# A fused decay attention and squared-ReLU MLP: lower halves kept in the next pair's place, row sums and the split of v moved

## The chip, the cores and the metric

The kernel runs on one core of a Trainium2 chip. The metric is device time in microseconds (us). Engines are named as in the profile: PE (TensorE matmul), PEld (its weight loads), DVE (VectorE), ACT (ScalarE), POOL (GpSimd) and SP (SyncE, which here only issues DMAs).

## The reference

Inputs are q, k, v of shape (8 batches, 8 heads, 576 positions, 64) and a forget factor f per position. Per head:

```
scores = q @ k.T / sqrt(D)
cum    = cumsum(log(clip(f, 1e-4, 1)))
scores = where(causal, -1e9, scores + cum[:, None] - cum[None, :])
attn   = softmax(scores)
out    = attn @ v
```

The heads' outputs side by side are x, 4608 tokens by 512, and the result is `relu(x @ w_in)**2 @ w_out` with 2048 hidden columns. All of it is float32.

## The kernel before, in words

**Two streams on one PE.** Attention is walked head by head (64 heads), each head in six units (`UNITS`, keys x queries): u0 is keys 0-127 with queries 256-575, u1 to u3 are the key tiles from 256, 384 and 512, u4 is keys 128-255 with queries 128-575, u5 is keys 0-127 with queries 0-255. One unit is one slot of the main loop (line 762), so a head has six slots. A slot traces `score` of its unit (matmuls into PSUM, exp on ACT, the triangle cut out by POOL's affine select), then `av_part` of the unit two slots earlier (LAG), then what `finish` and the table of events hold for it, and fills up with half steps of the MLP. Two heads make a pair, whose outputs fill the 128 partitions of one place of an `xt` tile; four pairs make a batch.

**The MLP** works on chunks of 256 tokens. One step is a hidden tile of 128: its first half, `mlp1`, is 12 matmuls of 256 columns, then on ACT a ReLU and two squares (`r`, `g`, `gh`), then on DVE the low part `gl`; its second half, `mlp2`, is six matmuls of 512 columns for the step before. `fill` (line 682) traces half steps at the middle and at the end of each slot, so many that their count keeps to a straight line. From `ready[b]`, the slot in which batch b's last pair is finished plus two, it goes from one batch's chunks to the next in 48 slots. Six of the seven lines (two chunks per batch) have 64 half steps for 48 slots: 4/3 per slot, so in three slots four of the six half slots hold a half step and two hold none. One batch has three chunks and two half steps in every slot. The last three chunks follow after the attention.

**From head 14 on** (`NWHOLE`) a probability tile is split into a high and a low part: `ph` (a cast on ACT, line 414), `pl` (a subtraction on DVE, 415). `sum_p` adds the tile to a running total on DVE (428), and after u4 and u5 `columns` reduces the total to row sums (434). The total is also the tile into which u0's and u5's exp writes. v is split likewise by `split_v`: a cast on DVE (321), then a subtraction on POOL (322).

**Row maxima.** Before a head's scores its row maxima are needed, six matmul and DVE pieces (`max_unit`, lines 336 and 342) traced in the head before, at the slots 2.5, 3, 3.5, 4, 4.5 and 5 (`MAXIMA`). A tile of 128 maxima goes by a 512-byte DMA on SP (line 347, `rk<-tcol`) into row 66 of the operand `r2` of the score matmul (line 381). The first score of a head, u0, reads the maxima of queries 256 to 575: the first three of the five DMAs. On the same SP stands `load` (line 250): the next head's q and k, 288 KB, into the only `qkraw` tile, which waits for POOL's last reading of it (line 314).

**Accumulators.** For a split head the output of ph times (v high, v low) has 128 rows, 64 high and 64 low. `av_part` copies the upper 64 rows into `xt` (line 502) and the lower 64 into `xl` (line 504), which is a single buffer named `den`. The accumulator itself is one PSUM bank, so the matmuls of the next part of a head (line 464) wait for both copies.

**Finishing a pair** (`finish`, at the slots of `DIVIDE` after the pair's last): the sums of both heads are stored to DRAM (454) and loaded back in another layout (526, part 0); part 1 adds `xl` to the pair's `xt` place (535), reduces and inverts the sums (537, 540) and stores them (542); part 2 loads them spread over the partitions into the tile `den` (549); part 3 multiplies (551, POOL). The `den` of part 2 and the `xl` of the pairs share the one buffer, and the next pair's first copy into `xl` comes two slots after part 3.

PE, ACT, DVE and POOL run in the order of tracing. SP's order is chosen by the Tile scheduler. A head starts at its u0 score; in what follows an even head opens a pair and an odd head closes it.

Of the kernel before, what the change touches and what calls it, by code (L numbers as in the profile page):

```python
# [9 lines left out]
F32 = mybir.dt.float32  # L10
# [26 lines left out]
def decay_attention_relu2_kernel(  # L37
# [277 lines left out]

    def split_v(h):
        if NWHOLE <= h < NH:
            st = state[h]
            vr = st["vr"][:, :, :D]
            v = st["vhl"] = vhls[h % 2]  # L320
            nc.vector.tensor_copy(out=v[:, :, :D], in_=vr)
            nc.gpsimd.tensor_tensor(
                out=v[:, :, D:], in0=vr, in1=v[:, :, :D].bitcast(F32), op=ALU.subtract,
            )

# [81 lines left out]
    def split_p(h, u):  # L407
        st = state[h]
        j, q0, q1 = UNITS[u]
        n = q1 - q0  # L410
        p = st["p"][u]
        ph = wk.tile([P, 448], F32R, name="ph", bufs=3)
        pl = wk.tile([P, 448], F32R, name="pl", bufs=3)
        nc.scalar.copy(out=ph[:, :n], in_=p[:, :n])  # L414
        nc.vector.tensor_tensor(  # L415
            out=pl[:, :n], in0=p[:, :n], in1=ph[:, :n].bitcast(F32), op=ALU.subtract,
        )
        st["p"][u] = ph, pl
        sum_p(h, u, p)

    def sum_p(h, u, p):

        st = state[h]
        _, q0, q1 = UNITS[u]
        total = totals[0]

        def add(p, q0, q1):
            nc.vector.tensor_tensor(  # L428
                out=total[:, q0:q1], in0=total[:, q0:q1], in1=p, op=ALU.add,
            )  # L430

        def columns(o, q0, q1):
            n = (q1 - q0) // 32
            nc.vector.tensor_reduce(
                out=st["sums"][:, o:o + n], in_=total[:, q0:q1].rearrange("p (i c) -> p c i", c=n),
                axis=mybir.AxisListType.X, op=ALU.add, apply_transpose=True,
            )

        if 0 < u < NU - 1:
            add(p[:, max(QA - q0, 0):q1 - q0], max(q0, QA), q1)  # L440
            if q0 < QA:
                st["rest"] = p[:, :QA - q0], q0, QA
        if u == NU - 2:
            st["sums"] = wk.tile([P, NC], F32, name="sums")
            columns(0, QA, S)
        if u == NU - 1:
            add(*st.pop("rest"))
            columns(NH1, 0, QA)

# [16 lines left out]
    def av_part(h, u, low):  # L466
# [21 lines left out]
        if last:  # L488
            n = QA if low else S - QA
            if not low:  # L490
                if h % H == 0:
                    xts[h // H] = wk.tile([P, NCC, S], F32, name=f"xt{h // H % 2}", bufs=1)
                if replicated(h):
# [4 lines left out]
                if h >= NWHOLE:  # L498
                    st["xl"] = state[h - 1]["xl"] if h % 2 else wk.tile([P, S], F32, name="den", bufs=1)
            o = (h % 2) * D  # L500
# [152 lines left out]

    DIVIDE = (2, 6, 9, 13), (2, 4, 5, 6)
    DIRECT = {1: 3, 3: 4}
# [5 lines left out]

    unsplit = []

# [4 lines left out]
    def fin(h, part):  # L668

        return (h + 1) * NU - 1 + (DIRECT if replicated(h) else DIVIDE[h >= H])[part]  # L670

# [48 lines left out]
    for h in range(NH):  # L720
        split = h >= NWHOLE
        if split:
            at((h - 2) * NU + LOAD, 1, load, h)
            at((h + 1) * NU, 1, store_sums, h)
            for part in range(4):
# [6 lines left out]
        at((h - 1) * NU + VLOAD[h == 0 or h >= H], 1, load_v, h)  # L732
        at((h - 1) * NU + VSPLIT, 1, split_v, h)
        for i, x in enumerate(MAXIMA[split]):
# [27 lines left out]
    for n in range(-2 * NU, last_slot + 1):  # L762
# [20 lines left out]
        cv(wr / 2)  # L783
        fill(n, 0.5)
        for do in events.get((n, 1), ()):
            do()
        cv(wr / 2)
        fill(n, 1.0)
    convert(1 << 20)
    while halves[0] < 2 * NCHUNK * NF:  # L790
# [43 lines left out]
```

## Time and profile before

| | |
|---|---|
| median of 3 runs | 1338.84 us (1337.23 to 1343.93) |
| the profiled execution, its time | 1343.43 us |
| its span, first to last instruction | 1341.6 us |
| mean granted TensorE clock in it | 0.961 |
| PE busy | 1195.9 us, 89% |
| DVE, ACT, POOL busy | 57%, 54%, 37% |
| attention ends, MLP alone after it | about 1198 us |

The profiled execution took 1.8 us more than its span, and lies 0.3% above the median. A row of the waits reads: engine, tile and line that stood still, what it waited for, us in total, times, longest. A row of the timeline reads: start, duration, engine, line, operation, tiles, then in brackets the idle time before it and what ended it. A row of the windows gives the stretch, its length, each engine's busy time, then the granted clock (1.00 is full speed) and the DMA share.

### The profile page before, as it was taken

What the parts mean: (1) busy time and instruction counts of PE and PEld (TensorE: products, weight loads), DVE (VectorE), ACT (ScalarE), POOL (GpSimd) and SP (SyncE); (2) the same over time, 40 slices, a digit from 0 to 9 for tenths busy, and PEclk for the clock granted to TensorE, in tenths of its full rate; (3) what the DMA queues carried; (4) which work ended last, traced back from release to release, by engine and by line L of the source; (5) the groups of instructions that cost most, each with busy time, mean ns of one, the idle gap of its engine ahead of it and who ended that gap; (6) DMA issues with size and microseconds to landing.
All of it is one profiled execution on the core that took longest, in us unless ns stands there. A gap on an engine that the chain in (4) does not pass through costs nothing.

```text
span 1341.6 us, 22717 instructions
## 1 busy us (share of the span) xinstructions
PE 1195.9 (89%) x7302; PEld 1054.3 (79%) x7302; DVE 765.4 (57%) x2032; ACT 724.8 (54%) x1908; POOL 490.2 (37%) x818
## 2 busy tenths in 40 slices
PE   4887999898888888989999888889888888889998
PEld 3556878787778778888898777778777877879997
DVE  7757655665666556656665655666566666631211
ACT  3655656555555555555655555555655455543443
POOL 4544453433444343433333434443434444300000
PEclk9988999988999999999999999999999899999999
DMA  7966624233423333332323324333343234100000
GB/s 190 190 154 170 165 47 94 57 66 74 89 61 71 75 74 67 63 84 50 81 67 57 80 52 89 74 68 66 64 90 74 67 65 90 37 26 1 17 16 17
DMA packets 136074, 101.88 MB, mean 76 GB/s; under 512 B 108408, under 2 KB 108408, under 8 KB 135956
## 3 DMA queue, kind: packets, MB, share of 16 engines
q1 hardware_dynamic: 122836, 66.80, 22.2%
q0 software_dynamic: 13120, 33.63, 12.2%
q8 instruction: 59, 0.97, 0.3%
q14 instruction: 59, 0.48, 0.1%
HBM read 89.85 MB, written 10.34 MB: 75 GB/s over the span
## 4 chain that ended last, share of the span: by engine, by line
PE 48%; DVE 18%; DMA 12%; issue 8%; ACT 6%; POOL 4%; SPq 3%; POOLq 0%; DVEq 0%; ACTq 0%
PE bank L581 20%; PE bank L604 17%; DMA den<-rdr 6%; DVE pl L415 5%; DVE bank L342 4%; PE bank L464 4%; DMA rk<-tcol 2%; POOL xt L551 2%; DVE wmag L428 2%; PE bank L485 1%; PE bank L375 1%; PE bank L381 1%; ACT r L589 1%; DVE xt L535 1%; ACT g L590 1%
## 5 line engine op out<-in xcount | busy, mean ns | idle before, releaser
L604 PE MATMUL bank<-w,gh 128*128 128x512 f32 x1152 | 423.4, 409 | 0.0
L581 PE MATMUL bank<-xh,w 128*128 128x256 f32 x2304 | 342.8, 292 | 7.8 <-DVE xh L568 4.2
L581 PEld LDWEIGHTS bank<-xh,w 128*128 128x128 f32 x2304 | 310.8, 195 | 15.6 <-issue 4.6
L592 DVE TENSOR_TENSOR gl<-g,gh 128x256 fp32r<-128x256 f32 x288 | 120.1, 417 | 256.2 <-ACT gh L591 255.4
L604 PEld LDWEIGHTS bank<-w,gh 128*128 128x128 f32 x1152 | 226.7, 197 | 40.9 <-ACT gh L591 0.3
L604 PE MATMUL bank<-w,gl 128*128 128x512 f32 x576 | 234.6, 407 | 3.5 <-DVE gl L592 3.5
L401 POOL TENSOR_SCALAR_AFFINE_SELECT p<-p 128x128 f32<-128x128 f32 x200 | 68.0, 340 | 406.9 <-ACT p L399 359.8
L589 ACT ACTIVATE r<-bank 128x256 f32<-128x256 f32 x288 | 110.4, 383 | 178.6 <-PE bank L581 175.5
L415 DVE TENSOR_TENSOR pl<-p,ph 128x320 fp32r<-128x320 f32 x200 | 138.8, 694 | 94.6 <-ACT ph L414 85.9
L581 PE MATMUL bank<-xl,w 128*128 128x256 f32 x1152 | 192.1, 291 | 0.0
L581 PEld LDWEIGHTS bank<-xl,w 128*128 128x128 f32 x1152 | 165.6, 199 | 0.0
L464 PE MATMUL bank<-ph,vhl 128*128 128x320 f32 (+4 forms) x350 | 108.1, 309 | 64.3 <-ACT den L504 64.3
L342 DVE CUSTOM_DVE_ANT_0 bank<-bank,mz 128x256 f32<-128x256 f32 (+4 forms) x320 | 130.8, 435 | 48.5 <-PE bank L336 46.9
L336 PE MATMUL bank<-rk 66*128 66x320 f32 (+9 forms) x384 | 116.9, 318 | 18.7 <-DMA rk<-qkraw 10.7
L604 PEld LDWEIGHTS bank<-w,gl 128*128 128x128 f32 x576 | 113.5, 197 | 19.5 <-DVE gl L592 5.4
L464 PEld LDWEIGHTS bank<-ph,vhl 128*128 128x128 f32 x350 | 68.4, 195 | 75.4 <-ACT den L504 71.5
L590 ACT ACTIVATE g<-r 128x256 f32<-128x256 f32 x288 | 120.4, 418 | 10.9 <-DVE gl L592 1.8
L414 ACT CAST ph<-p 128x320 fp32r<-128x320 f32 x200 | 81.2, 406 | 79.4 <-POOL p L401 78.8
L591 ACT ACTIVATE gh<-r 128x256 fp32r<-128x256 f32 x288 | 115.6, 401 | 0.0
L415 DVE TENSOR_TENSOR pl<-wmag,ph 128x320 fp32r<-128x320 f32 x100 | 49.5, 495 | 114.3 <-ACT ph L414 114.3
L381 PE MATMUL bank<-rk 67*128 67x320 f32 (+4 forms) x300 | 89.2, 297 | 25.8 <-DMA rk<-tcol 14.6
L399 ACT ACTIVATE p<-bank 128x320 f32<-128x320 f32 x200 | 75.9, 380 | 66.8 <-PE bank L384 59.4
(93 smaller groups left out, 1762.7 us busy)
## 6 DMA issues: line engine op xcount, KB each, us to landing
rk<-in_qk POOLq DMA_DIRECT2D x64, 288.0 KB, 3.9
qkraw<-in_qk SPq DMA_DIRECT2D x50, 288.0 KB
rl<-in_qk POOLq DMA_DIRECT2D x100, 144.0 KB, 4.1
out<-osb SPq DMA_DIRECT2D x36, 256.0 KB
v<-in_v SPq DMA_DIRECT2D x56, 160.0 KB
den<-rdr SPq DMA_DIRECT2D x62, 144.0 KB
w<-in_w_in SPq DMA_DIRECT2D x16, 512.0 KB
w<-in_w_out SPq DMA_DIRECT2D x16, 512.0 KB
```

The costliest lines, as they stand in the source:

```text
L336: nc.tensor.matmul(ps[:m, :n], st["r2"][:rows, q0:q0 + m], st["kl0"][:rows, k0:k0 + n], start=True, stop=True,)
L342: nc.vector.tensor_tensor_reduce(out=ps[:m, :n], in0=ps[:m, :n], in1=mz[:m, mo:mo + n], op0=ALU.add, op1=ALU.min, scale=-1.0, scalar=init, ...
L381: nc.tensor.matmul(ps[:kn, :n], st["kl0"][:D + 3, k0:k0 + kn], st["r2"][:D + 3, q0:q1], start=True, stop=False,)
L414: nc.scalar.copy(out=ph[:, :n], in_=p[:, :n])
L415: nc.vector.tensor_tensor(out=pl[:, :n], in0=p[:, :n], in1=ph[:, :n].bitcast(F32), op=ALU.subtract,)
L464: nc.tensor.matmul(*args, start=first and k == 0, stop=last and k == 1)
L581: nc.tensor.matmul(ph[:, :T], w[:, s, cc], x[:, cc, :], start=(cc == 0 and k == 0), stop=(cc == NCC - 1 and k == 2),)
L589: nc.scalar.activation(out=r, in_=ph[:, :T], func=AF.Relu)
L590: nc.scalar.activation(out=g, in_=r, func=AF.Square)
L591: nc.scalar.activation(out=gh, in_=r, func=AF.Square)
L592: nc.vector.tensor_tensor(out=gl, in0=g, in1=gh.bitcast(F32), op=ALU.subtract)
L604: nc.tensor.matmul(po, g[:, ts], w[:, s], start=(fc == 0 and k == 0), stop=(fc == NF - 1 and k == 2),)
```

## The change

Four edits, and the tables that go with them.

- `xl` lies no longer in `den` but in the place of the next pair in the `xt` tiles, which is free until that pair's first output comes.
- `DIVIDE` gets a third row for split heads: parts 0 to 3 at 3, 5, 6 and 8 slots behind the pair's last instead of 2, 4, 5 and 6 (heads 8 to 13: 2, 4, 6, 7). `ready` is counted from part 3, so the line of the MLP's half steps starts two slots later against the heads. `store_sums` is traced half a slot later.
- `sum_p` is traced behind the half steps in the middle of a slot instead of directly behind the split, and `columns` behind those at its end.
- `split_v` is traced in two: the DVE cast half a slot earlier, the POOL subtraction a slot later.

```diff
-    def split_v(h):
+    def split_v(h, low):
...
-            nc.vector.tensor_copy(out=v[:, :, :D], in_=vr)
-            nc.gpsimd.tensor_tensor(
-                out=v[:, :, D:], in0=vr, in1=v[:, :, :D].bitcast(F32), op=ALU.subtract,
-            )
+            if not low:
+                nc.vector.tensor_copy(out=v[:, :, :D], in_=vr)
+            else:
+                nc.gpsimd.tensor_tensor(
+                    out=v[:, :, D:], in0=vr, in1=v[:, :, :D].bitcast(F32), op=ALU.subtract,
+                )
...
         st["p"][u] = ph, pl
-        sum_p(h, u, p)
+        unsummed.append((h, u, p))
...
+        if u == NU - 1:
+            add(*st.pop("rest"))
+        if u >= NU - 2:
+            unreduced.append((h, u))
...
-                if h % H == 0:
-                    xts[h // H] = wk.tile([P, NCC, S], F32, name=f"xt{h // H % 2}", bufs=1)
+                pair = h // 2 + 1
+                for b in (h // H, pair // NCC if h >= NWHOLE else 0):
+                    if b not in xts:
+                        xts[b] = wk.tile([P, NCC, S], F32, name=f"xt{b % 2}", bufs=1)
...
                 if h >= NWHOLE:
-                    st["xl"] = state[h - 1]["xl"] if h % 2 else wk.tile([P, S], F32, name="den", bufs=1)
+                    st["xl"] = xts[pair // NCC][:, pair % NCC, :]
...
-    DIVIDE = (2, 6, 9, 13), (2, 4, 5, 6)
+    DIVIDE = (2, 6, 9, 13), (2, 4, 6, 7), (3, 5, 6, 8)
...
-            at((h + 1) * NU, 1, store_sums, h)
+            at((h + 1) * NU + 1, 0, store_sums, h)
...
-        at((h - 1) * NU + VSPLIT, 1, split_v, h)
+        at((h - 1) * NU + VSPLIT, 0, split_v, h, False)
+        at((h - 1) * NU + VSPLIT + 1, 1, split_v, h, True)
...
         fill(n, 0.5)
+        while unsummed:
+            sum_p(*unsummed.pop(0))
...
         fill(n, 1.0)
+        while unreduced:
+            columns(*unreduced.pop(0))
```

Three places show how instructions stand. Lines of the changed kernel are numbered a little higher (347 becomes 349, 381 becomes 383, 504 becomes 513). The first is PE in a two-chunk batch, from the third maximum (L336, 320 columns, `rk_69`) to the first score of the next head (L381, 320 columns, `rk_69`). L581 is mlp1, L604 is mlp2 (six rows, of which two are shown). Before:

```order
L336 MATMUL bank_5322<-rk_69 128x320
L581 MATMUL bank_5333<-xh_4049,w_858 128x256 x8
L581 MATMUL bank_5333<-xl_4050,w_858 128x256 x4
L336 MATMUL bank_5357<-rk_69 128x192
L604 MATMUL bank_5059<-w_798,gh 128x512
L604 MATMUL bank_5059<-w_798,gl 128x512
...
L381 MATMUL bank_5367<-rk_68 128x256
L384 MATMUL bank_5367<-rl 128x256
...
L581 MATMUL bank_5386<-xh_4049,w_977 128x256 x8
L581 MATMUL bank_5386<-xl_4050,w_977 128x256 x4
L381 MATMUL bank_5407<-rk_69 128x320
```

The same stretch of PE in the changed kernel, where L338 is the maximum, L590 mlp1, L613 mlp2 and L383 the score:

```order
L338 MATMUL bank_5287<-rk_69 128x320
L338 MATMUL bank_5292<-rk_69 128x192
L590 MATMUL bank_5300<-xh_4090,w_747 128x256 x8
L590 MATMUL bank_5300<-xl_4091,w_747 128x256 x4
L383 MATMUL bank_5321<-rk_68 128x256
L386 MATMUL bank_5321<-rl 128x256
...
L613 MATMUL bank_5095<-w_675,gh 128x512
L613 MATMUL bank_5095<-w_675,gl 128x512
...
L383 MATMUL bank_5352<-rk_69 128x320
```

Three half steps stood between the two, and two stand there now. It is so at the start of the heads 18 to 33 and 42 to 63 (38 heads).

The second place is SP, around the maxima of an odd head (`rk_69`) in a two-chunk batch. Before:

```order
L542 DMA rdr<-sums 2x32x10
L542 DMA rdr<-sums 2x32x8
L347 DMA rk_69<-tcol 1x128x1 x3
L250 DMA qkraw<-in_qk 64x1152
L549 DMA den<-rdr 64x576 x2
L347 DMA rk_69<-tcol 1x128x1
L347 DMA rk_69<-tcol 1x64x1
```

The same place in the changed kernel, with the maxima of the even head after it (`rk_68`) behind it:

```order
L349 DMA rk_69<-tcol 1x128x1 x2
L250 DMA qkraw<-in_qk 64x1152
L551 DMA rdr<-sums 2x32x10
L551 DMA rdr<-sums 2x32x8
L349 DMA rk_69<-tcol 1x128x1 x2
...
L558 DMA den<-rdr 64x576 x2
L459 DMA sdr<-sums 4x32x18
...
L349 DMA rk_68<-tcol 1x128x1 x2
L250 DMA qkraw<-in_qk 64x1152
L349 DMA rk_68<-tcol 1x128x1 x2
```

The third maximum of an odd head stood ahead of the load of qkraw and stands behind it now, and behind the two stores of `rdr`. Of the 19 even heads among the 38, nine have it behind qkraw, as nearly all even heads had before. The other ten, at the end of a chunk, have both stores of the MLP's result among the first maxima, and the load behind:

```order
L349 DMA rk_68<-tcol 1x128x1
L620 DMA out<-osb 128x512
L349 DMA rk_68<-tcol 1x128x1
L620 DMA out<-osb 128x512
L349 DMA rk_68<-tcol 1x128x1 x2
L250 DMA qkraw<-in_qk 64x1152
```

The third place is ACT at the start of a head: u0's exp into the total, the two copies of the accumulator, the split. Before, at the start of an odd head:

```order
L399 ACTIVATE wmag_2252<-bank5_6371 128x320 [waits PE_49]
L502 COPY xt1_4924<-bank0_6204 64x320 [waits PE_49]
L504 COPY den_6377<-bank0_6204 64x320 [waits DMAHW7_49,DMAHW6_49,Pool_49]
L414 CAST ph_6380<-wmag_2252 128x320 [waits Activation_49]
L399 ACTIVATE p_6400<-bank1_6397 128x320 [waits PE_49]
```

And in the changed kernel:

```order
L401 ACTIVATE wmag_2246<-bank5_6072 128x320 [waits DVE_49,PE_49]
L511 COPY xt1_4393<-bank0_5918 64x320 [waits PE_49]
L513 COPY xt1_4393<-bank0_5918 64x320
L416 CAST ph_6080<-wmag_2246 128x320 [waits Activation_49]
L598 ACTIVATE r_6097<-bank4_6084 128x256 [waits PE_49]
```

The second copy waits for POOL and two DMAs no more. The exp has a wait for DVE that it had not: `columns` of the head before.

More of the change, by code (lines that the diff above doesn't have):

```diff
@@ L430, in add @@
             )
[L432 to L437, printed above, removed]
         if 0 < u < NU - 1:
@@ L442, in sum_p, with columns @@
                 st["rest"] = p[:, :QA - q0], q0, QA
+        if u == NU - 1:
+            add(*st.pop("rest"))
+        if u >= NU - 2:
+            unreduced.append((h, u))
+    def columns(h, u):
+        st = state[h]
         if u == NU - 2:
             st["sums"] = wk.tile([P, NC], F32, name="sums")
[L445 to L448, printed above, removed]
+        o, q0, q1 = (0, QA, S) if u == NU - 2 else (NH1, 0, QA)
+        n = (q1 - q0) // 32
+        nc.vector.tensor_reduce(
+            out=st["sums"][:, o:o + n], in_=totals[0][:, q0:q1].rearrange("p (i c) -> p c i", c=n),
+            axis=mybir.AxisListType.X, op=ALU.add, apply_transpose=True,
+        )
     def store_sums(h):
@@ L660, in decay_attention_relu2_kernel @@
     slots = [(h, u) for h in range(NH) for u in range(NU)]
-    unsplit = []
+    unsplit, unsummed, unreduced = [], [], []
     def split_last():
@@ L668, in fin @@
     def fin(h, part):
-        return (h + 1) * NU - 1 + (DIRECT if replicated(h) else DIVIDE[h >= H])[part]
+        return (h + 1) * NU - 1 + (DIRECT if replicated(h) else DIVIDE[(h >= H) + (h >= NWHOLE)])[part]
     avs = {}
```

## The prediction

> **What bounds the kernel now.** I read the page first, then the list of waits, the busy time by stage, and the timeline at the places that the waits named. The list of waits (who waited <- for whom: us in total, times, longest):
>
> ```profile
> POOL xt L551 <- DMA den<-rdr: 75.0, 27, 17.3
> ...
> PE bank L464 <- ACT den L504: 64.3, 25, 3.4
> ...
> ACT den L504 <- POOL xt L551: 32.4, 20, 3.0
> ...
> PE bank L381 <- DMA rk<-tcol: 14.6, 11, 2.0
> ...
> PE bank L604 <- DVE gl L592: 3.5, 5, 2.2
> ```
>
> PE is the bound, and what it loses it loses mostly at one place: line 464 waits for a copy of the accumulator, which waits for POOL's multiplication, which waits for the DMA that brings `den`. Second comes the score that waits for row maxima. By stage (us, busy time of each engine, granted clock):
>
> ```profile
> 306.18:573.24 267.06, 234.38 (x1456) 211.87 (x1456) 161.79 (x446) 147.74 (x399) 109.72 (x176) 0.94 0.35 71
> 615.39:745.37 129.98, 128.66 (x842) 115.88 (x841) 79.44 (x203) 77.91 (x208) 47.16 (x76) 1.00 0.32 66
> 789.41:1165.48 376.07, 331.22 (x2079) 300.45 (x2080) 232.97 (x640) 209.80 (x566) 157.35 (x251) 0.95 0.35 72
> 1220.00:1320.00 100.00, 100.00 (x642) 90.81 (x641) 16.91 (x38) 40.78 (x109) 0.00 (x0) 1.00 0.03 11
> ```
>
> The three-chunk batch (second row) and the MLP's tail (fourth) keep PE 99 to 100% busy at full clock; there is nothing to gain or lose in them. The two-chunk batches idle, and their clock is lower. The third row runs from one multiplication of POOL to the tenth after it:
>
> ```profile
> L551 POOL TENSOR_TENSOR xt<-xt,den x11: 1395/1396/1442, 789.4 to 1165.5; 128x576 f32<-128x576 f32 x11
> ```
>
> So a pair takes 37.6 us, of which PE idles (376.07 - 331.22) / 10 = 4.5 and loses 0.05 x 37.6 = 1.9 to the clock; 31.2 is work. The first row, seven pairs of 38.15, gives 31.2 too (4.7 idle, 2.3 clock).
>
> The first copy of an odd head, on the timeline:
>
> ```profile
> 863.77 1.40 POOL L551 TENSOR_TENSOR xt<-xt,den 128x576 f32<-128x576 f32 x1 [2.12 <-DMA den<-rdr]
> ...
> 865.20 0.42 ACT L504 COPY den<-bank 64x320 f32<-64x320 f32 x1 [1.44 <-POOL xt L551]
> ...
> 865.67 0.39 PE L464 MATMUL bank<-ph,vhl 128*128 128x256 f32 x1 [2.88 <-ACT den L504]
> ...
> 866.19 1.37 PE L581 MATMUL bank<-xh,w 128*128 128x256 f32 x8
> ```
>
> And the start of an even head. The third maximum (875.44) must reach SP by way of DVE, stands there behind `qkraw`, which waits for POOL's line 314, and the score at 882.16 waits for its landing:
>
> ```profile
> 874.83 0.37 PE L381 MATMUL bank<-rk 67*128 67x448 f32 x1
> ...
> 875.44 0.33 PE L336 MATMUL bank<-rk 66*128 66x320 f32 x1
> 875.61 1.12 PE L581 MATMUL bank<-xh,w 128*128 128x256 f32 x8
> ...
> 876.49 1.42 POOL L314 TENSOR_TENSOR rl<-qkraw,rk 64x576 fp32r<-64x576 f32 x1
> 876.57 0.64 PE L581 MATMUL bank<-xl,w 128*128 128x256 f32 x4
> 876.62 0.52 DVE L342 CUSTOM_DVE_ANT_0 bank<-bank,mz 128x320 f32<-128x320 f32 x1
> ...
> 877.14 0.42 PE L604 MATMUL bank<-w,gh 128*128 128x512 f32 x1
> ...
> 877.94 0.53 SPq L250 DMA_DIRECT2D qkraw<-in_qk  x1
> ...
> 878.56 0.55 SPq L347 DMA_DIRECT2D rk<-tcol  x1
> ...
> 880.03 0.64 PE L581 MATMUL bank<-xl,w 128*128 128x256 f32 x4
> ...
> 882.16 0.38 PE L381 MATMUL bank<-rk 67*128 67x320 f32 x1 [1.49 <-DMA rk<-tcol]
> ```
>
> **The clock.** Busy time and granted clock around the gaps:
>
> ```profile
> 867.00:870.40 3.40, 3.40 (x14) 2.92 (x13) 1.32 (x3) 1.63 (x5) 0.04 (x1) 0.50 0.89 187
> 919.38:921.08 1.70, 0.00 (x1) 0.03 (x1) 0.54 (x5) 0.40 (x2) 1.49 (x3) 1.00 0.24 43
> 921.60:925.00 3.40, 3.40 (x12) 2.81 (x11) 1.72 (x4) 2.15 (x6) 0.59 (x2) 0.50 1.25 217
> ...
> 882.20:885.60 3.40, 3.40 (x22) 3.12 (x23) 1.90 (x5) 3.16 (x9) 1.04 (x3) 1.00 1.08 210
> ```
>
> After the gap of 2.88 us, and after one of 1.70, PE runs 3.4 us at half clock, which costs 1.7; after the gap of 1.49 it does not. The Trainium skill has it otherwise (TensorE: Matmul & The Clock Gate, section "HAM oscillation — how this bites in real kernels"): only gaps above some 3.4 us are to be avoided. The trace disagrees; the rule is a rival below.
>
> **The change part by part.** *The lower halves.* The copy no longer waits for POOL, so the 2.88 us and the half clock behind it go, 4.6 us of a pair. What is late next decides the forecast.
>
> *The shift of the MLP by two slots* takes one of three half steps from between the third maximum and the next score, at 38 starts. A half step is 877.14 - 875.61 = 1.53 us on PE. The other chain keeps its length: from the score of u4 (874.83) by exp, POOL's select and line 314 to SP, it ended 7.33 us later. PE was there after 5.84 (880.67); now after 4.31. The wait of 1.49 becomes 3.0. This holds for the nine even heads whose third maximum stays behind `qkraw`.
>
> *Odd heads* had no wait there:
>
> ```profile
> 855.57 1.11 SPq L542 DMA_DIRECT2D rdr<-sums  x2
> ...
> 856.78 1.80 SPq L347 DMA_DIRECT2D rk<-tcol  x3
> ...
> 860.36 0.31 PE L381 MATMUL bank<-rk 67*128 67x320 f32 x1
> ```
>
> The third of the three was issued at about 858.06 (the last 0.5 of 1.80) and the score ran 2.30 later without waiting. In the change it stands behind `qkraw` (0.62 from its issue to the next in the even head) and two `rdr` (1.11): issued 1.73 behind `qkraw`, on the even head's times at 879.67. With 2.30 from issue to score, the undisturbed case, the wait would be 2.8; with the 3.60 of the even head (878.56 to 882.16), where `qkraw` had just been issued, 4.1. I take 3.05, near the lower end, since 1.1 of qkraw's head start is gone. DVE makes part 1 and the cast of v ahead of that maximum now; this can lengthen it and is in the upper end.
>
> *Ten even heads with the stores of the MLP's result.* Nothing of before shows two of them ahead of a third maximum:
>
> ```profile
> qkraw<-in_qk SPq DMA_DIRECT2D x50, 288.0 KB
> ...
> out<-osb SPq DMA_DIRECT2D x36, 256.0 KB
> ```
>
> The maximum is through DVE at 877.28 (0.52 and 0.14 for reading it, after 876.62). Undisturbed it would be there at 879.58, a wait of 0.4; behind a store issued 0.55 earlier and nearly as large as `qkraw`, at about 881.4, a wait of 2.3. I take the middle, 1.3, without half clock.
>
> *The sums, v, store_sums, part 1 to 3.* DVE does the same instructions, the low parts sooner. `columns` now comes just ahead of u0's exp, 0.72 us in the mean of its two widths:
>
> ```profile
> L434 DVE TRANSPOSE_TENSOR_REDUCE sums<-wmag 128x10 f32<-128x320 f32 x100 | 72.0, 720 | 3.4
> ```
>
> While the score waits 3 us for its maxima this is hidden; if it did not wait, I would charge up to 0.7 us per start, 27 us in all. The later POOL subtraction frees POOL's queue, which stood still for the cast, but line 314 hangs on the select of u4 and so on PE's score: nothing comes of it there. POOL's multiplication, a slot later against its DMA, should no longer wait; with that the longest wait of line 604 for `gl` (the 2.2 in the first fence) may go, 3.9 together with a half clock; I count half. At the end PE waits for the last batch's x:
>
> ```profile
> 1198.61 2.05 PE L581 MATMUL bank<-xh,w 128*128 128x256 f32 x8 [4.15 <-DVE xh L568]
> ```
>
> One more slot of MLP (1.33 half steps) stands ahead of it: 2 us less.
>
> **The sum**, over 19 pairs. Before: 8 at 38.15 and 11 at 37.6 are 719 us. After: work 19 x 31.2 = 593; waits 19 x 3.05 + 9 x 3.0 + 10 x 1.3 = 98; half clock behind the 28 long waits 28 x 1.7 = 48; together 739, 20 more. Less 2 for line 604 and 2 at the end, 16 more. The profiled execution took 1343.43; 1359 on its terms, and 1354 on those of the median (1338.84, 0.34% below it).
>
> **The rivals.**
>
> *The maxima come in time* (the other side). If the load of `qkraw` were issued earlier, since POOL no longer stands still, the 28 long waits would stay at 1.5, below what costs clock. Each saves 1.55 + 1.7: 91 us, 1264. For it: POOL stood idle 2.12 us at 863. Against: line 314 started 1.66 us after the score of u4, with nothing of `den` in that stretch. It decides where the landing comes 1.5 us sooner. 12 in 100.
>
> *Gaps of 3 us leave the clock alone*, if they fall otherwise against the windows in which it is granted: 48 us less, 1307. Against it stand the 0.50 behind gaps of 2.88 and 1.70. By the Trainium skill's rule named above it would be so for every gap. 8 in 100.
>
> *The SP queue is worse than I take it.* Odd starts wait 4.1 and the ten even ones 2.3 with half clock: 19 x 1.05 + 10 x (1.0 + 1.7) = 47 more, 1401. For it: part 1 ahead of the maximum on DVE. 10 in 100.
>
> *The forecast*, odd and even starts waiting about 3 us: 60 in 100. Its lower end: odd 2.8, the ten even 0.4, three quarters of the clock cost, 5 + 9 + 12 = 26 less, 1328; its upper end half of the rival above, 1378. The other 10 in 100 are causes that I do not see, on all sides.
>
> **The numbers.** 1354 is the likeliest. 1305 to 1385 leaves out the first rival (12) and most of the third. A measurement of this kernel tells about 0.5% from no change, so slower is above 1345.5: three quarters of the forecast (45), the third rival (10) and 3, 58 in 100. Faster, below 1332: 12 + 8 and 3 each of the forecast's lower end and of the unseen, 26. The same: 16.
>
> **What would show it.** The wait of line 464 for a copy should be gone, and the wait of the score (383 there) for `rk<-tcol` stand first in PE's list, at about 90 us; POOL's wait for `den` should be short; the two-chunk stages should show 5 us of PE idle a pair and a clock of 0.93 to 0.95, with two half-clock windows in most pairs. It is wrong if PE's waits there sum to less than 60 us, if the score's longest wait is near 1.5, or if another line leads the list.

## The result

| | median | range | runs |
|---|---|---|---|
| before | 1339.19 us | 1337.23 to 1343.93 | 4 |
| after | 1355.65 us | 1351.35 to 1356.07 | 4 |

The ratio is 1.0105, with a 95% interval of 1.0077 to 1.0133: the change makes the kernel about 14 us slower. The profiled execution of after took 1356.07 us (span 1354.4, mean granted clock 0.962). Medians of before shift by a few us from one set of runs to the next, so each experiment below is given as a ratio to the runs of before made beside it.

**The profile after.** In the list of waits (us in total, times, longest), line 383 (before's 381) leads PE's waits under three names, since the landing of the maxima is put down to whatever finished nearest to it:

```profile
PE bank L383 <- DMA rk<-tcol: 40.2, 19, 3.8
...
PE bank L383 <- DVE sums L450: 32.9, 11, 3.4
...
POOL xt L560 <- DMA den<-rdr: 32.7, 13, 17.3
...
PE bank L383 <- DMA rk<-cum_dr: 16.3, 5, 3.3
```

The group of that line on the page has the sum, 92.8 us of idle time:

```profile
L383 PE MATMUL bank<-rk 67*128 67x320 f32 (+4 forms) x300 | 91.6, 305 | 92.8 <-DMA rk<-tcol 40.2
...
L469 PE MATMUL bank<-ph,vhl 128*128 128x320 f32 (+4 forms) x350 | 107.6, 307 | 9.9 <-ACT xt L513 9.8
```

The wait for the copy (64.3 us in before) is down to 9.8, and POOL's wait for `den` from 75.0 to 32.7, of which 17.3 is the last pair's. By stage, again from multiplication to multiplication (seven pairs, the batch of three chunks, nine pairs):

```profile
304.12:579.38 275.26, 237.50 (x1455) 214.79 (x1454) 174.24 (x449) 148.69 (x397) 111.62 (x176) 0.93 0.37 69
620.02:750.24 130.22, 128.05 (x841) 115.61 (x841) 79.00 (x203) 79.03 (x209) 46.80 (x76) 1.00 0.34 66
791.31:1148.38 357.07, 307.40 (x1875) 276.99 (x1874) 224.56 (x579) 191.77 (x513) 143.53 (x227) 0.93 0.37 69
```

A pair of the last row takes 39.7 us: (357.07 - 307.40) / 9 = 5.5 idle, 0.07 x 39.7 = 2.8 lost to the clock, 31.4 work. Before it was 4.5, 1.9 and 31.2. From here on "the two-chunk stages" are the stretches from the start of head 18 to that of head 34 and from that of head 42 to that of head 63. They take 703.8 us in the profiled execution of before and 729.7 in that of after.

Two starts of after on the timeline. An odd one: DVE makes part 1 (lines 546, 549) and the cast of v (322) ahead of the third maximum, which PE had done at 856.3; SP issues qkraw and two rdr ahead of it, and the score starts 3.48 late:

```profile
855.28 0.37 PE L383 MATMUL bank<-rk 67*128 67x448 f32 x1
...
855.90 0.42 PE L338 MATMUL bank<-rk 66*128 66x320 f32 x2
...
856.83 0.30 DVE L546 TENSOR_REDUCE sums<-parts 64x18 f32<-64x90 f32 x1
...
857.35 1.44 DVE L322 CAST vhl<-v 128x320 fp32r<-128x320 f32 x1
...
858.60 0.52 SPq L250 DMA_DIRECT2D qkraw<-in_qk  x1
...
858.71 0.48 DVE L344 CUSTOM_DVE_ANT_0 bank<-bank,mz 128x320 f32<-128x320 f32 x1
...
859.21 1.14 SPq L551 DMA_DIRECT2D rdr<-sums  x2
...
860.45 1.79 SPq L349 DMA_DIRECT2D rk<-tcol  x3
...
863.20 0.39 PE L383 MATMUL bank<-rk 67*128 67x320 f32 x1 [3.48 <-DMA rk<-tcol]
```

An even one without stores of the result. DVE has the third maximum at 877.62 (877.48 and 0.14), but SP, waiting for POOL to free `qkraw`, issues it at 879.75, and the score starts 3.84 after that:

```profile
877.48 0.14 DVE L344 DVE_READ_ACCUMULATOR2_ANT tcol<- 128x1 f32 x1
...
877.70 1.42 POOL L314 TENSOR_TENSOR rl<-qkraw,rk 64x576 fp32r<-64x576 f32 x1
...
879.14 0.52 SPq L250 DMA_DIRECT2D qkraw<-in_qk  x1
...
879.75 1.19 SPq L349 DMA_DIRECT2D rk<-tcol  x2
...
883.59 0.39 PE L383 MATMUL bank<-rk 67*128 67x320 f32 x1 [3.15 <-DMA rk<-tcol]
```

And an even one with stores. The scheduler has the third maximum ahead of `qkraw` there; it is issued at 840.74 and the score runs 2.17 later without a wait:

```profile
840.10 0.55 SPq L620 DMA_DIRECT2D out<-osb  x1
...
840.74 1.13 SPq L349 DMA_DIRECT2D rk<-tcol  x2
...
841.97 0.55 SPq L250 DMA_DIRECT2D qkraw<-in_qk  x1
...
842.91 0.39 PE L383 MATMUL bank<-rk 67*128 67x320 f32 x1
...
845.64 0.44 ACT L401 ACTIVATE wmag<-bank 128x320 f32<-128x320 f32 x1 [2.19 <-DVE sums L450]
```

Here the exp of u0 comes only 2.73 behind the score, since it waits for `columns` of the head before. The copies stand behind it on ACT, and all nine of line 469's waits for a copy (9.8 us) lie in such heads.

### The profile page after: what moved, and what is told of

Read it like the earlier page. It is cut to its first block, busy times and chain, and to the rows that moved or that the text cites. A ratio compares the mean times of both kernels' runs of the same rounds, so it can differ in the third digit from the quotient of the medians.

```text
span 1354.4 us, 22801 instructions
## 1 busy us (share of the span) xinstructions
PE 1197.4 (88%) x7302; PEld 1053.3 (78%) x7302; DVE 790.7 (58%) x2032; ACT 729.5 (54%) x1908; POOL 496.4 (37%) x818
## 4 chain that ended last, share of the span: by engine, by line
PE 58%; DVE 19%; DMA 9%; ACT 6%; issue 5%; POOL 1%; SPq 1%; POOLq 0%; ACTq 0%; DVEq 0%
PE bank L590 25%; PE bank L613 19%; PE bank L469 5%; DVE bank L344 3%; DVE pl L417 3%; DMA rk<-tcol 3%; DVE vhl L322 2%; PE bank L383 2%; PE bank L338 2%; PE bank L386 2%; DMA rl<-tcol 2%; DVE gl L601 2%; DVE sums L450 1%; DVE wmag L430 1%; ACT r L598 1%
## 5 line engine op out<-in xcount | busy, mean ns | idle before, releaser
L613 PE MATMUL bank<-w,gh 128*128 128x512 f32 x1152 | 418.9, 404 | 0.0
L590 PE MATMUL bank<-xh,w 128*128 128x256 f32 x2304 | 347.6, 296 | 6.8 <-DVE tcol L344 3.1
L590 PEld LDWEIGHTS bank<-xh,w 128*128 128x128 f32 x2304 | 320.0, 200 | 15.1 <-ACT r L598 3.6
L601 DVE TENSOR_TENSOR gl<-g,gh 128x256 fp32r<-128x256 f32 x288 | 133.4, 463 | 279.7 <-ACT gh L600 278.1
L613 PEld LDWEIGHTS bank<-w,gh 128*128 128x128 f32 x1152 | 222.8, 193 | 40.6 <-ACT gh L600 0.3
L403 POOL TENSOR_SCALAR_AFFINE_SELECT p<-p 128x128 f32<-128x128 f32 x200 | 63.4, 317 | 475.2 <-ACT p L401 471.2
L613 PE MATMUL bank<-w,gl 128*128 128x512 f32 x576 | 230.0, 399 | 0.0
L590 PE MATMUL bank<-xl,w 128*128 128x256 f32 x1152 | 194.6, 294 | 0.0
L383 PE MATMUL bank<-rk 67*128 67x320 f32 (+4 forms) x300 | 91.6, 305 | 92.8 <-DMA rk<-tcol 40.2
L590 PEld LDWEIGHTS bank<-xl,w 128*128 128x128 f32 x1152 | 168.6, 202 | 0.0
L383 PEld LDWEIGHTS bank<-rk 67*128 67x128 f32 (+1 forms) x300 | 55.0, 183 | 117.5 <-DVE sums L450 82.6
L344 DVE CUSTOM_DVE_ANT_0 bank<-bank,mz 128x256 f32<-128x256 f32 (+4 forms) x320 | 132.3, 428 | 20.7 <-PE bank L338 19.2
L338 PE MATMUL bank<-rk 66*128 66x320 f32 (+9 forms) x384 | 110.7, 317 | 21.1 <-DMA rk<-qkraw 10.7
L613 PEld LDWEIGHTS bank<-w,gl 128*128 128x128 f32 x576 | 112.1, 195 | 15.1 <-DVE gl L601 1.1
L401 ACT ACTIVATE wmag<-bank 128x320 f32<-128x320 f32 x100 | 40.2, 402 | 133.6 <-PE bank L386 112.9
```

What stands on the lines that cost most here:

```text
L338: nc.tensor.matmul(ps[:m, :n], st["r2"][:rows, q0:q0 + m], st["kl0"][:rows, k0:k0 + n], start=True, stop=True,)
L344: nc.vector.tensor_tensor_reduce(out=ps[:m, :n], in0=ps[:m, :n], in1=mz[:m, mo:mo + n], op0=ALU.add, op1=ALU.min, scale=-1.0, scalar=init, ...
L383: nc.tensor.matmul(ps[:kn, :n], st["kl0"][:D + 3, k0:k0 + kn], st["r2"][:D + 3, q0:q1], start=True, stop=False,)
L401: nc.scalar.activation(out=p[:kn, :n], in_=ps[:kn, :n], func=AF.Exp, scale=SCALE)
L590: nc.tensor.matmul(ph[:, :T], w[:, s, cc], x[:, cc, :], start=(cc == 0 and k == 0), stop=(cc == NCC - 1 and k == 2),)
L601: nc.vector.tensor_tensor(out=gl, in0=g, in1=gh.bitcast(F32), op=ALU.subtract)
```

## The experiments

The prediction has two causes for the score's waits: the shift takes PE work from between the third maximum and the score, and in odd heads the maximum comes to stand behind `qkraw` and two rdr on SP. The experiments ask how much each is worth. The rival to the shift: what holds the maximum is SP's order, in even heads too, and work on PE matters only behind that.

**Half steps later in after** (first and second run), and the change's parts put into before (third and fourth). In the first two and the fourth the shift holds for the first batch too, which the change leaves alone there.

```diff
 # after, e1 (e2: + 4)
-    ready = [fin(b * H + H - 1, 3) + 2 for b in range(B)]
+    ready = [fin(b * H + H - 1, 3) + 3 for b in range(B)]
 # before, e3 and e4
-                    st["xl"] = state[h - 1]["xl"] if h % 2 else wk.tile([P, S], F32, name="den", bufs=1)
+                    st["xl"] = xts[pair // NCC][:, pair % NCC, :]
 # before, e4 only
-    ready = [fin(b * H + H - 1, 3) + 2 for b in range(B)]
+    ready = [fin(b * H + H - 1, 3) + 4 for b in range(B)]
```

> The kernel after with the MLP's half steps begun one slot later (ready + 3 in place of + 2): three half steps instead of two stand again between the third row maximum and the next score, as in the kernel before; everything else is as after. Theory 'too little PE work between maximum and score': each of the 28 long score waits (mean 3.1 us) loses one half step, 1.53 us, and is left at about 1.6, at the edge of what costs half clock: 28 x 1.53 = 43 to 28 x (1.53 + 1.7) = 90 us less than after's 1356, so 1266 to 1313, PE's idle before line 383 near 45. Rival 'the chain behind the maximum is late by itself' (DVE's moved sums, v's low part on POOL, two rdr stores on SP stretch along with the added work): the waits stay at 3 us and the time within 15 us of 1356. Rival 'the sums of a row now stand in front': the waits fall, but columns in front of u0's exp costs 0.7 us at each of 38 starts, 27 us, and the time lies at the upper end, above 1300, with waits of line 469 or 401 in place of the score's.

Measured: 1377.26 us, ratio 1.0298 (1.0254 to 1.0341). With a half step more, the kernel is some 25 us slower by the ratios, not 43 or more faster, and an odd start still waits 3.40:

```profile
870.44 0.37 PE L383 MATMUL bank<-rk 67*128 67x448 f32 x1
...
872.02 0.55 ACT L401 ACTIVATE p<-bank 128x448 f32<-128x448 f32 x1 [1.56 <-DVE wmag L430]
...
875.08 0.52 SPq L250 DMA_DIRECT2D qkraw<-in_qk  x1
...
876.94 1.58 SPq L349 DMA_DIRECT2D rk<-tcol  x2
...
879.67 0.42 PE L383 MATMUL bank<-rk 67*128 67x320 f32 x1 [3.40 <-DMA rk<-tcol]
```

From the score of u4 to the next head's start it is 879.67 - 870.44 = 9.23 here, 863.20 - 855.28 = 7.92 in after: the chain grew by 1.31 of the half step's 1.53. The exp of u4 starts 1.58 behind the score here and 0.62 in after; it waits for the sum on DVE (line 430), which the change moved. SP's order changed as well. The ten even heads with stores have the third maximum ahead of `qkraw` in after, and behind it here:

```profile
856.62 0.52 SPq L250 DMA_DIRECT2D qkraw<-in_qk  x1
857.23 0.55 SPq L349 DMA_DIRECT2D rk<-tcol  x1
...
860.57 0.39 PE L383 MATMUL bank<-rk 67*128 67x320 f32 x1 [2.27 <-DVE xl L578]
```

These ten starts wait 2.1 in the mean where they waited 0.1; the nine other even ones wait 2.6 instead of 3.0. So the "late by itself" rival has the mechanism of the odd starts right (though not its time, within 15 us of 1356), and the run is no clean test of a half step: it moves SP's order too.

> The kernel after with the half steps begun two slots later (ready + 4): three half steps between third maximum and score, and two instead of one behind the last maximum. Theory 'too little PE work between maximum and score': as in the run with one slot, 1266 to 1313; if the last two maxima (not the third) set the landing, it beats that run by up to 28 x 1.5 us. Rival 'the third maximum alone counts': the two runs agree within 10 us. Rival 'the chain is late by itself': within 15 us of 1356.

Measured: 1399.31 us, ratio 1.0447 (1.0398 to 1.0497). None of the expectations: 44 us slower than after. As in e1 nearly every third maximum (37 of 38) is behind `qkraw`; odd starts wait 5.0 in the mean, even ones 2.0.

> The kernel before with one part of the change: the lower halves go to the next pair's place. DIVIDE, sums, v and the half steps' phase are as before. Theory: the 25 waits of line 464 for the copy (64.3 us) go, and the half clock behind 17 or 18 of them (1.7 us each, 30 us); the score's waits of 14.6 us stay: 1339 - 94 = 1245, with PE's idle before the score below 25. Rival 'what the copy waited for was cover for the row maxima': the waits move to the score, the gain is under 40 us, 1300 or above.

Measured: 1324.65 us, ratio 0.9887 (0.9854 to 0.9921), 15 us gained of 94 expected. PE's waits:

```profile
PE bank L464 <- ACT xt L506: 29.9, 23, 1.7
PE bank L381 <- DMA rk<-tcol: 21.1, 14, 2.5
PE bank L336 <- DMA rk<-in_qk: 19.2, 14, 2.1
```

The time is as the rival had it (1300 or above), but the waits do not move to the score as it said: those are 27 us in the two-chunk stages, 24 in before. Line 464 still waits for the copy itself, some 1.3 us a time, and the maxima's first matmul (336) waits 19.2 for `in_qk`, which it hardly did in before.

> The run with the lower halves alone, and the half steps begun two slots later (ready + 4 in the kernel before), which gives the change's phase: two half steps between third maximum and score. DIVIDE, sums and v as before, so on SP the third maximum of an odd head stays ahead of qkraw. Theory 'the phase is the loss': even starts wait 3.0 instead of 1.5 with half clock behind (19 or fewer x 3.2 = up to 61 us more than the run with the lower halves alone), odd starts between 0 and 1.5 (up to 28 more): 1275 to 1335 if that run gives 1245, and what is missing to 1356 is the place of the odd head's third maximum behind qkraw and two rdr. Rival 'the phase does nothing, DIVIDE and the sums do': within 10 us of the run with the lower halves alone.

Measured: 1308.66 us, ratio 0.9776 (0.9742 to 0.981). The shift, expected to cost up to 89 us, gains 16. It does lengthen the waits of the score, from 27 us in the two-chunk stages to 72 (28 of them 1.7 to 3.1 each), and it ends the waits of lines 464 and 336 there, 55 us together. In these stages it so comes out even, 687.9 us without it and 685.3 with it; half of the gain, 9 us, lies ahead of head 18, where this run shifts the first batch too. In an odd start here it is den that stands ahead of the third maximum, which DVE has at 866.60:

```profile
866.47 0.13 DVE L342 DVE_READ_ACCUMULATOR2_ANT tcol<- 128x1 f32 x1
...
867.07 1.16 SPq L551 DMA_DIRECT2D den<-rdr  x2
...
868.27 1.23 SPq L347 DMA_DIRECT2D rk<-tcol  x2
...
871.38 0.39 PE L381 MATMUL bank<-rk 67*128 67x320 f32 x1 [2.32 <-DVE pl L415]
```

The rest of the change (the division, the sums, v) therefore costs the 3.3% between this ratio and after's, 44 us. They all lie in the two-chunk stages (685.3 us here, 729.7 in after): 15 more of the score's waits, 10 of line 469's, and 20 more lost to half clock.

**One thing changed in after at a time.**

```diff
 # e5: SP's order alone ("third" is the DMA that line 349 issues for the third maximum)
         nc.sync.dma_start(out=qkraw[:D], in_=qk[h])
+        tc.add_manual_dep(tc.nc.cur_bb.bb.instructions[-1], state[h - 1]["third"], mybir.DependencyInfo(
+            mybir.DependencyClass.NoSync, mybir.DependencyReason.DATA), reason="the third maximum first")
 # e6
-    DIVIDE = (2, 6, 9, 13), (2, 4, 6, 7), (3, 5, 6, 8)
+    DIVIDE = (2, 6, 9, 13), (2, 4, 6, 7), (3, 4, 5, 6)
-    ready = [fin(b * H + H - 1, 3) + 2 for b in range(B)]
+    ready = [fin(b * H + H - 1, 3) + 2 + 2 * (b > 0) for b in range(B)]
 # e7
-        at((h - 1) * NU + VSPLIT, 0, split_v, h, False)
+        at((h - 1) * NU + VSPLIT, 1, split_v, h, False)
 # e8
-        unsummed.append((h, u, p))
+        sum_p(h, u, p)
-            unreduced.append((h, u))
+            columns(h, u)
```

> The kernel after with one thing in SP's order: the load of qkraw is issued behind the third row maximum's rk<-tcol, which it stands ahead of in after at the 28 long waits. Nothing else is moved. Theory 'the third maximum is held on SP behind qkraw, which waits for POOL, and lands slowly beside it': in an even head of after DVE has the third maximum at 877.6, SP issues it at 879.75 and the score starts at 883.59; issued at 877.7 it lands near 880.1, before PE is there (880.4), so the 10 even waits (3.1 and 1.7 of half clock each, 48 us) go. In an odd head DVE has it only at 821.8 (part 1 and the cast of v stand ahead), the landing is near 824.2 and PE there at 822.3: 1.9 is left of 3.3, 18 x 1.4 = 25 us, and up to 31 more if half clock does not follow a gap of 1.9. Together 1356 - 73 = 1283, down to 1252. Rival 'too little PE work between maximum and score' (the forecast's step): the waits stay, since no half step is added; within 15 us of 1356. Rival 'the wait moves to the next user of the queue (prep of the head after waits for its qkraw)': at most 20 us less.

Measured: 1288.1 us, ratio 0.9618 (0.9592 to 0.9644); 1283 was expected. No half step and no arithmetic is moved, and 65 us go: of the starts' 87 us in the two-chunk stages 46 are left, none over 2.3, and the half clock there lasts 17 us instead of 92. So SP's order is shown as the cause of these 65 us. An even start without stores; DVE has the third maximum at 839.32:

```profile
839.19 0.13 DVE L350 DVE_READ_ACCUMULATOR2_ANT tcol<- 128x1 f32 x1
...
839.36 1.11 SPq L355 DMA_DIRECT2D rk<-tcol  x2
...
840.56 0.55 SPq L250 DMA_DIRECT2D qkraw<-in_qk  x1
...
841.50 0.38 PE L391 MATMUL bank<-rk 67*128 67x320 f32 x1 [1.53 <-DMA rk<-tcol]
```

SP issues it 0.04 later and the score starts 2.14 behind the issue, 3.84 in after. The odd starts still wait 1.7 in the mean, with SP no longer the cause: at head 47 DVE has the maximum at 822.12, behind part 1 and the cast of v, and SP issues it at 822.15. PE's list:

```profile
PE bank L391 <- DVE tcol L350: 25.9, 16, 1.8
PE bank L391 <- DMA rk<-tcol: 13.0, 10, 2.2
```

> The kernel after with the parts of the division back a slot (3, 4, 5, 6 in place of 3, 5, 6, 8; part 0 stays, since the sums' store lies later now), and the half steps begun at the same slots as in after. Sums and v as in after. On SP rdr is then issued before u4 and the odd head's order is den, den, third maximum, qkraw. Theory 'what stands ahead of the third maximum on SP and DVE': the odd head's maximum no longer waits for part 1 on DVE nor for qkraw and rdr on SP, but for den, as in the run with lower halves and shift, where odd starts wait 2.3: 18 x 1.0 = 18 us, and up to 31 of half clock, less than 1356: 1307 to 1338. Even starts as in after. Rival 'the sums' move is what the kernel after loses against lower halves and shift (1309)': within 10 us of 1356.

Measured: 1350.82 us, ratio 1.0096 (1.0066 to 1.0125), level with after (1.0105). With the parts earlier, den stands ahead of the odd maximum in place of qkraw and rdr, and the long waits of the starts are still 2.2 to 3.7; the odd starts wait 2.6 in the mean instead of 3.1.

> The kernel after with the cast of v's upper part behind the maxima of its slot again (the second half of u4; the lower part stays one slot later). Theory 'SP holds the third maximum': in an odd head DVE has it 1.4 us sooner, but on SP it still stands behind qkraw (issued 821.19) and two rdr, so the waits stay: within 10 us of 1356. Rival 'the cast ahead of the maximum makes it late': 18 odd waits lose 1.4 each, 25 us, and 10 even ones some of it: 1331 or below.

Measured: 1359.89 us, ratio 1.0167 (1.0134 to 1.02). Not faster: at head 47 DVE has the maximum 2.6 behind the score of u4 instead of 4.0, and that is worth nothing while SP holds it.

> The kernel after with the sums of a row and columns traced where before has them (right behind the split of p); store_sums, v, the division and the half steps as in after. Theory 'SP holds the third maximum': the long waits stay, and columns no longer stands ahead of u0's exp, which the wait hides anyway: within 10 us of 1356. Rival 'the sums' new place delays the exp of u4 by the buffers of p (its two buffers are held until the sum has read them), and with it POOL's line 314, qkraw and the maximum': ACT's wait for L430 (35.3 us, 37 times) goes, the 28 waits lose about 1 us each: 1328 or below, and the place of the sums explains most of the 47 us between after and the run with lower halves and shift.

Measured: 1363.91 us, ratio 1.02 (1.0166 to 1.0234). Not faster, but not because `columns` cost nothing: in the ten even heads with stores u0's exp comes 0.6 to 1.0 behind the score again (2.7 to 4.1 in after), and of line 469's 10 us in the two-chunk stages 0.4 are left. More is lost at the odd starts, where nine waits, a third of the long ones, last 4.9 to 6.0; why is not shown. Undone one by one, none of the three parts gives back the 44 us that they cost together; how they share it stays open.

**SP's order set, with and without the shift.** e9 is the run with lower halves and shift, with the order of e5, part 2 and 3 a slot later, and both den<-rdr behind the third maximum too; e10 is the same with the half steps one slot later, which is three slots later than in before: the pattern repeats every three slots, so before's three half steps stand between maximum and score again; e11 is e5 with a half step more; e12 is the run with lower halves and shift with the order of e5 alone.

```diff
 # e9 and e10, on e4's and e3's lower halves
-    DIVIDE = (2, 6, 9, 13), (2, 4, 5, 6)
+    DIVIDE = (2, 6, 9, 13), (2, 4, 6, 7)
                 nc.sync.dma_start(out=den[i * D:(i + 1) * D], in_=st["rdr"][i:i + 1].broadcast_to([D, S]))
+                tc.add_manual_dep(tc.nc.cur_bb.bb.instructions[-1], state[h + 2]["third"], mybir.DependencyInfo(
+                    mybir.DependencyClass.NoSync, mybir.DependencyReason.DATA), reason="the third maximum first")
-    ready = [fin(b * H + H - 1, 3) + 2 for b in range(B)]
+    ready = [fin(b * H + H - 1, 3) + 2 + 1 * (b > 0) for b in range(B)]
 # e10: + 2 * (b > 0) there; e11, on e5: + 1 * (b > 0)
```

> The run with lower halves and shift (1308.7), with SP's order set: the third row maximum ahead of qkraw, and, in the odd heads, ahead of the two den<-rdr, for which part 2 and part 3 come one slot later (2, 4, 6, 7); the half steps begin where that run has them. Sums, v and the rest as in the kernel before. Theory 'the third maximum is held on SP': in that run's odd head DVE has it at 866.6, SP issues it at 868.27 behind den, and the score starts at 871.38; issued at 866.6 it lands near 869.0, when PE is there (869.06). So even and odd waits go (68.5 us of line 381 in the two-chunk stages, and 51 us of half clock, half of it lost): 94 us less, against up to 20 us of new short waits for copies (1.4 each, as the run with the third maximum before qkraw shows): 1215 to 1240. Rival 'something else of the chain is late by then' (exp, POOL): 1270 or above.

Measured: 1243.02 us, ratio 0.9326 (0.9302 to 0.9349), faster than both kernels and 3 us above what the theory gave. An odd start, issued in time, needs no wait (the third of the three DMAs goes out at 863.00, and 2.1 later the score runs):

```profile
861.75 1.80 SPq L353 DMA_DIRECT2D rk<-tcol  x3
...
863.65 0.54 SPq L559 DMA_DIRECT2D den<-rdr  x1
...
865.11 0.39 PE L389 MATMUL bank<-rk 67*128 67x320 f32 x1
...
865.52 0.60 SPq L250 DMA_DIRECT2D qkraw<-in_qk  x1
```

Nine pairs of the later two-chunk stage, as in the windows above:

```profile
768.66:1068.66 300.00, 285.30 (x1871) 256.29 (x1870) 236.11 (x582) 191.78 (x515) 149.73 (x225) 0.99 0.39 82
```

A pair takes 33.3 us, of which 1.6 is idle.

> The same kernel as the run with lower halves, shift and maxima first, but the half steps begun where the kernel before has them (three half steps between third maximum and score, two in the other). Theory 'the slot of the half steps sets other waits': the waits of line 464 for ACT's copy (38 us in the two-chunk stages of the run with the lower halves alone, 1.45 each) and of line 336 for in_qk (19 us) stay, only line 381's 24 us go: near 1295, 55 or more slower than the run with the shift. Rival 'with SP mended, three half steps cover more than two': faster than the run with the shift. Rival 'the phase does nothing once SP is mended': the two within 10 us.

Measured: 1294.92 us, ratio 0.9715 (0.9689 to 0.9741), as the first theory had it. With before's three half steps the score hardly waits (1.8 us in the two-chunk stages), but the two other waits are there again:

```profile
PE bank L472 <- ACT xt L514: 49.5, 40, 1.5
PE bank L342 <- DMA rk<-in_qk: 31.1, 20, 2.5
```

> The kernel after with the third maximum before qkraw (1288.1), and the half steps of all batches but the first begun one slot later: three half steps instead of two between third maximum and score. Theory 'PE work covers the wait once SP's order does not move with it': the odd waits left (43 us of line 383 in 28 waits in the two-chunk stages, 1.5 each) go: 1288 - 43 = 1245, or 1250 with the shorter clock loss kept. Rival 'an added half step puts its own instructions into the queues ahead of the maximum (as in the run with one slot later, which lost 21 us)': 1288 or above.

Measured: 1258.97 us, ratio 0.9435 (0.9412 to 0.9458), some 25 us less than e5 by the ratios. Line 391's waits in the two-chunk stages go from 46 us to 31. So a half step does cover the wait of the even starts, once the maximum is not held on SP: theirs go from 14 us to 0.2. The odd ones stay at 1.6 to 1.7, since their chain grows with the half step as in e1, from 6.1 to 7.4; that is what the expectation lacks.

> The run with lower halves and shift (1308.7), with only qkraw behind the third maximum on SP; part 2 is not moved, so in an odd head den<-rdr stays ahead of the maximum. Theory 'SP's order, part by part': the even waits go (about 14 of 28, 2.8 each with half clock behind most: 39 + 20 = 59), the odd ones (2.3) stay: near 1250, and what the run with both mended gains beyond it is the place of den. Rival 'den's place costs nothing': equal to the run with both mended within 5 us.

Measured: 1267.43 us, ratio 0.9505 (0.9484 to 0.9527). The theory's halves come apart as it said: the nine long even waits are gone, the 19 odd ones stay, 2.4 us in the mean. It came to 1250 by counting 14 even ones. The place of den, and parts 2 and 3 with it, is worth the 1.8% between this ratio and e9's.

The runs side by side, each from its profiled execution: the time of the two-chunk stages, how long PE ran at half clock in them, and the mean wait of the score at the 19 odd starts, at the nine even starts whose third maximum is behind `qkraw` in after, and at the ten others (all in us).

| run | stages | half clock | odd | nine even | ten even |
|---|---|---|---|---|---|
| before | 703.8 | 75 | 0.1 | 1.3 | 1.0 |
| after | 729.7 | 92 | 3.1 | 3.0 | 0.1 |
| e1 | 742.0 | 109 | 3.6 | 2.6 | 2.1 |
| e2 | 763.9 | 133 | 5.0 | 2.1 | 1.9 |
| e3 | 687.9 | 41 | 0.1 | 1.2 | 1.4 |
| e4 | 685.3 | 51 | 2.4 | 2.8 | 0.2 |
| e5 | 665.0 | 17 | 1.7 | 0.9 | 0.6 |
| e6 | 726.7 | 76 | 2.6 | 3.0 | 0.1 |
| e7 | 736.4 | 99 | 3.5 | 2.9 | 0.1 |
| e8 | 736.0 | 109 | 4.1 | 3.0 | 0.1 |
| e9 | 621.8 | 3 | 0.3 | 0.0 | 0.1 |
| e10 | 669.0 | 7 | 0.1 | 0.0 | 0.0 |
| e11 | 635.9 | 7 | 1.6 | 0.0 | 0.0 |
| e12 | 648.1 | 29 | 2.4 | 0.0 | 0.1 |

## Why the prediction was right, and where its reason was wrong

The time was right (1354 forecast, 1355.65 measured) and the profile looked as described: line 464's wait gone, line 383 first with 92.8 us (90 forecast), 5.5 idle a pair (5), clock 0.93. By its own steps:

- *The lower halves.* In after the copy's wait is nearly gone, as forecast, but the lower halves alone do not do it: alone (e3) they left some 1.3 a time for the copies and a new wait for `in_qk`, and gained 15 us. Only the shift took these away (e4).
- *The shift.* Its effect on the score was read rightly. Over the nine even heads the stretch from the score of u4 to the start is 7.2 us in before and 7.4 in after, so the other chain did keep its length there, and the wait grew from 1.3 to 3.0; the shift alone (e3 to e4) takes it from 1.2 to 2.8. What failed is to charge the shift with that wait and credit it with nothing: it also ends the waits of lines 464 and 336, 55 us against 45, so that in the two-chunk stages it costs nothing there, and with SP's order mended it is worth 47 us (e10 to e9).
- *What holds the maximum.* The prediction's own rows have the third maximum behind `qkraw`, which waits for POOL's line 314, and so for the score of u4, exp and select. It took this as given in even heads and asked only how much work covers it. e5 shows that the order itself is worth 65 us. Before says so too: its four even starts with the third maximum ahead of `qkraw` (heads 22, 26, 54 and 58) did not wait, the 15 others waited 1.5 in the mean.
- *Odd heads.* Right in mechanism and nearly in size: 3.05 taken, 3.1 measured, behind `qkraw` and two rdr. With the order mended (e5) 1.7 is left, and at head 47 it is DVE that is late then.
- *Ten even heads with stores.* Mis-sized: 1.3 taken, 0.1 measured. The third maximum is ahead of `qkraw` there, and a store of 256 KB issued 0.64 before it did not slow it (2.17 from issue to score).
- *columns.* The price was put only on starts where the score does not wait, up to 0.7 each, and then left out of the sum. The ten even heads turned out to be such starts: line 469 waits for the copies there, 9.8 us in nine waits, and only 0.4 in e8.
- *Half clock.* 48 us forecast; after has 92 us at half clock in the two-chunk stages, so 46 lost.
- *The total.* Between the same multiplications of POOL, 17 pairs took 24 us more than before, where the forecast had 20 for 19 pairs. The rest of the kernel gave back 12 where it had 4: 2 ahead of the first of them, 4 in the three-chunk batch and around it, 5 at the end. That 1354 is within 2 us of the median is therefore partly luck: the misses, these and those of the single steps, cancel.

Of the rivals, *the maxima come in time* looked in the wrong direction (`qkraw` earlier); later is what brings them in time, e5 and e9. *Gaps leave the clock alone* fell: 24 of after's 27 gaps of 2.7 us and more in the two-chunk stages were followed by half clock. *SP is worse* did not come.

What stays open: how the 44 us divide among the division, the sums and v, why the odd chain is as long as it is in e2 and in nine heads of e8, and what the odd starts of e5 would gain from a free DVE.

## What to carry to other kernels

When a wait is for a small DMA, look first at what is issued ahead of it on the same queue, and at what that waits for; to count the work that covers it comes second, since the chain behind the queue may stretch with the work. Where a scheduler chooses a queue's order, a dependency without a wait can put the urgent small transfer first; here that order alone was worth 65 us. An edit that moves work moves a chosen order with it, as e1 did, so read the order again in every run. And a forecast of the right size whose cause is only half right is found out only by undoing the cause.

## What the runs showed of the hardware

Over all fourteen traces, take the starts of the two-chunk stages (and head 63) at which the score waited over 0.2 us, and measure from SP's issue of the third maximum, 512 bytes, to the score. With neither `qkraw`, den nor a store issued in the 3 us ahead of it, that is 2.1 us in the median (65 starts, 2.0 to 3.0). With the 288 KB load of `qkraw` issued less than 1 us ahead it is 3.5 (107 starts, 3.0 to 4.2), 1 to 3 us ahead 2.8 (97 starts, 2.0 to 5.5), and behind two den<-rdr 3.0 (57 starts, 2.5 to 3.8). Behind a 256 KB store it is 2.2 (16 starts, 2.0 to 3.4). The Trainium skill has a rule that fits (DMA: Bandwidth & Descriptors, section "Queues, rings and completion order"): the signal that a transfer is done is written only after every earlier write of the same DMA engine. The delays behind `qkraw` and den agree with it, but no run shows the engines one by one, nor whether it is the data or the signal that is late, and the store ahead did not delay the maximum.

The half clock has no sharp threshold in the length of a gap: the longer the gap, the more often it followed. Of the gaps on PE in the two-chunk stages (and head 63) of all fourteen traces, a stretch at half clock began, at the latest 3.4 us behind the gap's end, in 8% of those of 1.0 to 1.7 us (16 of 198), 46% of 1.7 to 2.7 (49 of 107), 79% of 2.7 to 3.1 (65 of 82), 95% of 3.1 to 3.4 (38 of 40) and all 51 longer ones. What decides is how much of the gap falls into one window of time. Within each trace all stretches at half clock begin on one grid of 3.413 us, to within 3 ns. Cut by this grid, the same stages show an edge: after a window with 1.9 us or more of PE idle time the next one was at half clock in 196 of 196 cases, after 1.6 to 1.9 in 40 of 84, and after less in 15 of 2621, eleven of which only go on with a half clock that was already there. Two gaps of the run with lower halves and shift, on its grid; the first, of 2.94 us, lies in one window, the second, of 2.35, is divided between two:

```profile
849.00:852.41 3.41, 0.52 (x3) 0.54 (x4) 2.60 (x8) 0.40 (x1) 1.86 (x4) 1.00 0.98 216
852.41:855.82 3.41, 3.41 (x17) 3.31 (x16) 0.49 (x1) 2.08 (x5) 0.00 (x0) 0.50 0.62 95
...
941.16:944.57 3.41, 2.29 (x15) 1.71 (x13) 3.38 (x6) 1.66 (x6) 2.76 (x3) 1.00 0.31 87
944.57:947.99 3.42, 2.19 (x17) 2.21 (x18) 3.33 (x8) 1.76 (x5) 2.60 (x3) 1.00 0.36 87
```

The first window is idle for 2.89 us and the next runs at half clock. The other two are idle for 1.12 and 1.23, and no half clock follows. So a gap of some 2 to 3 us costs or not by where it falls, which no forecast from lengths alone can tell.
